# One DMA transpose over 128 partitions and output products in 64x64 tiles for units 3 to 9 of a linear-attention kernel

## The chip, the cores and the metric

The kernel runs on one core of a Trainium2 chip. The core has a matrix engine (TensorE, PE in the profile; its weight loads are listed apart as PEld), VectorE (DVE), ScalarE (ACT), GpSimd (POOL), and SyncE (SP), which here issues most of the DMA transfers. Sixteen DMA engines move the data. The metric is the device time of one execution in microseconds.

## The reference

Two stages follow each other. The first is a gated recurrent attention for 4 sequences of 768 tokens and 8 heads of 48 channels; the state of each head decays by alpha, channel by channel:

```python
for t in range(S):
    state = alpha[:, :, t, :, None] * state + np.einsum('bhd,bhe->bhde', k[:, :, t], v[:, :, t])
    y[:, :, t] = np.einsum('bhd,bhde->bhe', q[:, :, t], state)
```

The second takes y as 3072 rows of 384 channels through a dense pair of layers of 2048 hidden units, with the square of the positive part between them:

```python
h = x @ w_in
r = np.maximum(h, 0.0)
g = r * r
return (g @ w_out).astype(np.float32)
```

Inputs and output are float32; the matrix products inside the kernel run on bfloat16.

## The kernel before

The work is cut into twelve units g of 256 tokens, numbered from 0: unit g is stretch i = g // 4 of sequence g % 4, so units 0 to 3 begin their sequences and units 8 to 11 end them. Within a unit, the partitions hold 128 pairs of neighbouring tokens; j (or jk, for keys) is the place in the pair. A unit has two chunks c of 64 pairs, which lie on partitions 0 to 63 and 64 to 127. Heads go by pairs: p (or n) counts four pairs, x (or rr) the head in the pair.

The steps of a unit, by the names that the prediction uses:

- **Loads** lda, ldk, ldq, ldv (L460): alpha, keys, queries, values, mostly issued by SP.
- **Front**: VectorE multiplies neighbouring alphas (L567), ScalarE takes logarithms (L570), TensorE sums them along the tokens (m1i, L576). From these sums come decay factors, which scale keys and queries into the tile QKS (qks in the profile; L643 and L638). QKS has [side a: keys or queries][j][head][64], 2048 columns on 128 partitions.
- **Transposes** tr0 and tr1 (L654): from unit 3 on, SP issues two DMA transposes, one for each chunk, that is, for 64 partitions by 2048 columns, into KQT (kqt). Each chunk's part of KQT has 1024 columns. KQT has three buffers.
- **Scores** p (L874): products of keys with queries in 64x64 tiles, into psX and psZ, and behind them in the same step the products of keys with values for the state (L727), also in 64x64 tiles with 48 columns. In the last stretch L727 is done for chunk 0 alone. p waits for both transposes.
- **Masks** mk (L891, VectorE): the causal scores into PM (pm).
- **Output** y (L762 and L754): the masked scores with the values ("products", L762), and the queries with the held state ("states", L754). Here a matmul's stationary operand has 64 rows and 128 columns, the 128 tokens of a chunk, and the moving one 48 columns. The row half is that of the chunk for the products and that of the head x for the states. Heads and chunks with x equal to c go to psX, the others to psZ. A unit has 32 products and 16 states; a unit that begins its sequence has 8 states, as chunk 0 has no state before it.
- **Transpose xt** (L932): from unit 4 on, SP transposes the result (128 partitions, 768 columns) for the dense layers; before, TensorE does (L926).
- **Dense layers**: s1 (L989, 128x256 matmuls, six to a step), the positive part (L997) and its square (L1007) on ScalarE, VectorE and GpSimd, s2 (L1035, 128x384 matmuls, four to a step), and the store (L1051).

The order of the work on each engine is written out by hand in TABLES (L206): one list of names for each of the five engines. A planner walks through it, finds for each step the earlier steps that it depends on, and places semaphore waits. SP's list mixes loads, transposes and stores, and SP issues them strictly in that order: a transfer that has to wait holds back all that stand behind it. TensorE's list mixes the attention steps of one unit with the dense steps of earlier ones.

TensorE may run neighbouring matmuls of different row halves side by side. The order in y keeps neighbours on alternating row halves, and a semaphore (swap) holds back the last states until the first products have been added up, since there the row halves change banks.

Of the kernel before, what the change touches and what calls it, by code (L numbers as in the profile page):

```python
# [26 lines left out]
class Program:  # L27
# [145 lines left out]
    def emit(self):  # L173
# [85 lines left out]
        bk5 sd4 vc5 bk6 sd5 sq5_1 vc7 sq8_1 vc10  # L259
    """,  # L260
    "sp": """
        lda0 ldk0 ldq0 ldv0 lda1 ldk1 ldv1 ldq1 lda3 ldk3 ldq3 lda4 ldv3 ldk4 ldq4 ldv4 tr0_3 tr1_3 lda5 tr0_4
        out0_1 tr1_4 ldk5 ldq5 ldv5 lda6 ldk6 tr1_5 tr0_5 out2_1 xt4 ldq6 out1_1 ldv6 lda7 ldq7 ldk7 tr0_6 tr1_6
        xt5 ldv7 out3_1 lda8 ldk8 tr0_7 tr1_7 out4_1 xt6 ldq8 ldv8 lda9 ldq9 ldk9 tr0_8 tr1_8 xt7 ldv9 lda10
        out5_1 ldk10 tr0_9 tr1_9 out6_1 xt8 ldq10 ldv10 lda11 ldk11 tr0_10 tr1_10 out7_1 xt9 ldq11 ldv11 tr0_11
        tr1_11 xt10 out8_1 xt11 out9_1 out10_1 out11_0 out11_10 out11_11
    """,
}
# [18 lines left out]
def bass_gla_recurrent__then__act_relu_squared_kernel(  # L287
# [328 lines left out]
    def front(g):  # L616
        b, i = units[g]
        t0 = i * T
        p0 = FRONT.get(g, (g - 1) * P)
        if g in BY_HEADS:  # L620
            front_by_heads(g, p0)
            return
        r, la, qs, kt, pm, vb, x2 = (g % n for n in (NRAW, 2, NQKS, NKQT, NPM, NV, 2))
        first, last = i == 0, i == NST - 1
        sr, sw = 2 * b + i % 2, 2 * b + (i + 1) % 2

        if g in BY_TOKEN:
# [14 lines left out]
        for a, E, key in ((0, EK, "ek"), (1, EQ, "eq"))[:1 if g in ROW_TILED else 2]:  # L642
            add("dve", lambda e, a=a, E=E: e.tensor_tensor(  # L643
                QKS[qs][:, a, :, :, 0:D], RAW[r][:, 1 + a].rearrange("p h j d -> p j h d"),
                E[la][:].rearrange("p j (h d) -> p j h d", h=H), ALU.mult),
                dve_ns(2 * HD), p0 + 1500 + 100 * a, reads=[("raw", r, 1 + a), (key, la, 0), (key, la, 1)],
                writes=[("qks", qs, a)], name=f"{key}m{g}")

        if g >= PE_TRANSPOSED:

            for c in range(2):
                src = QKS[qs][64 * c:64 * c + 64].rearrange("p a j h d -> p (a j h d)")
                dst = transposed(kt, c).rearrange("p (b s) -> p b s", s=64)
                add("sp", lambda e, dst=dst, src=src: e.dma_start_transpose(dst, src), 1300, p0 + 2500 + c,  # L654
                    reads=[("qks", qs, 0), ("qks", qs, 1)], writes=[("kqt", kt, 0, c), ("kqt", kt, 1, c)], name=f"tr{c}_{g}",
                    dma=f"t{c}_{kt}", lag=1700)
            return

        for a in range(2):
            src = QKS[qs][:, a].rearrange("p j h d -> p (j h d)")  # L660
            bank = psZ[:, a, :].bitcast(BF16)
            psk = [("ps", "Z", a)]

            def tr(pe, src=src, bank=bank):
                for o in range(2 * NPR):
                    ins = pe.matmul(bank[:, o * 128:(o + 1) * 128], src[:, o * 128:(o + 1) * 128], IDENT[:],
                                    is_transpose=True)
                return ins

            add("pe", tr, pe_ns(8, 128), p0 + 2500 + a, reads=[("qks", qs, a), ("ident",)], writes=psk,  # L670
                name=f"tr{a}_{g}")
            dst = KQT[kt][:].rearrange("p a j n s -> p (a j n s)").rearrange("p (c a o s) -> p a o c s", c=2, a=2, s=64)[:, a]
            at = bank.rearrange("p (o c s) -> p o c s", c=2, s=64)
            add("dve", lambda e, dst=dst, at=at: e.tensor_copy(dst, at), dve_ns(1024, 2),
                p0 + 3000 + a, reads=psk, writes=[("kqt", kt, a)], name=f"et{a}_{g}",
                alts={"act": (lambda e, dst=dst, at=at: e.activation(dst, at, AF.Copy), act_ns(1024))})
    def transposed(kt, c):
        return KQT[kt][:].rearrange("p a j n s -> p (a j n s)")[:, c * 1024:c * 1024 + 1024]

    def queries(kt, c, n):  # L680
        return transposed(kt, c)[:, 512 + n * 128:512 + n * 128 + 128]

    def names(g):
        b, i = units[g]
# [55 lines left out]
    def output_row_tiled(g):  # L740


        b, i, sr, sw = names(g)
        kt, pm, vb, x2 = g % NKQT, g % NPM, g % NV, g % 2
        first = i == 0

        def to(p, x, c):
            return psX[:, c, p * D:p * D + D] if x == c else psZ[:, c, p * D:p * D + D]

        def states(pe, tiles, start):  # L750
            for p in range(NPR):
                for x, c in tiles:
                    held = (SMD[x2] if c else SBD[sr])[64 * x:64 * x + 64, p * D:p * D + D]
                    ins = pe.matmul(to(p, x, c), queries(kt, c, p)[64 * x:64 * x + 64], held, start=(start and p == 0),  # L754
                                    stop=False, skip_group_check=True)
            return ins

        def products(pe, tiles, start):
            for p in range(NPR):
                for jk in range(2):  # L760
                    for x, c in tiles:
                        ins = pe.matmul(to(p, x, c), PM[pm][64 * c:64 * c + 64, p // 2, x, p % 2, jk, :],  # L762
                                        VBF[vb][64 * c:64 * c + 64, 2 * p + x, jk, :],
                                        start=(p == 0 and jk == 0 and (start or (first and c == 0))), stop=True,
                                        skip_group_check=True)
            return ins

        def run(pe):
            products(pe, ((1, 0), (0, 1)), True).then_inc(swap, 1)
            swaps[0] += 1  # L770
            states(pe, ((1, 1),) if first else ((0, 0), (1, 1)), True)
            products(pe, ((0, 0), (1, 1)), False)
            pe.wait_ge(swap, swaps[0])
            return states(pe, ((0, 1),) if first else ((0, 1), (1, 0)), False)

        reads = [("pm", pm, 0), ("pm", pm, 1), ("vbf", vb), ("kqt", kt, 1), ("smd", x2)] + ([] if first else [("sbd", sr)])
        return run, 620, reads, [("ps", bank, c) for bank in "XZ" for c in range(2)]
# [75 lines left out]
    def scores(g):  # L853
# [5 lines left out]
        def tiles(hfs):  # L859
            def run(pe):  # L860
                for hf in hfs:
                    psT = halves[hf][0]
                    for nn in range(2):
                        for jk in range(2):
                            for c in range(2):
                                for rr_ in range(2):
                                    n = 2 * hf + nn
                                    o = (nn * 2 + jk) * 128
                                    d0 = 64 * rr_
                                    mov = (queries(kt, c, n)[d0:d0 + 64] if g in ROW_TILED else  # L870
                                           KQT[kt][d0:d0 + 64, 1, :, n, 64 * c:64 * c + 64])
                                    keys = (transposed(kt, c)[d0:d0 + 64, (jk * NPR + n) * 64:(jk * NPR + n) * 64 + 64]
                                            if g in ROW_TILED else KQT[kt][d0:d0 + 64, 0, jk, n, 64 * c:64 * c + 64])
                                    ins = pe.matmul(psT[64 * c:64 * c + 64, rr_, o:o + 128], keys, mov)  # L874
                return ins
            return run
# [238 lines left out]
```

## Time and profile before

| what | value |
|---|---|
| median of 3 runs | 171.86 us (171.46 to 174.43) |
| the profiled execution, whole | 173.53 us |
| its span in the trace | 171.8 us |
| granted TensorE clock, mean | 1.0 |
| DMA transposes issued, L654 and L932 | 18 and 8 |
| matmuls | 2377 |
| output matmuls, L762 and L754 | 352 and 152 |

The profile follows one execution. Its page has the engines' busy time, a strip of 40 equal slices of the span (a digit is the busy share in tenths), the chain of work that ended last, and the costliest groups. Other answers of the trace are used too: a timeline (start, length, engine, line, operation, written tile <- read tiles, shapes, count; in brackets the idle time of the engine just before and what ended it), and the instructions of one line with the time from a DMA's issue to its landing. The end of a matmul in the trace is modelled and overlaps the next one, so its length is no price; the price of a matmul is the distance between starts. L numbers are lines of the kernel before.

### The profile page before, as it was taken

Reading aid. Unit: us, or ns where it says so; the run is one execution under the profiler, and the core shown is the slowest. Engines: PE = TensorE matmul, PEld = TensorE weight load, DVE = VectorE, ACT = ScalarE, POOL = GpSimd, SP = SyncE. Lnnn points to the kernel's source line nnn. Section 1 sums busy time; section 2 is a strip of 40 time slices with the busy share of each in tenths; the row PEclk is TensorE's granted clock in tenths of the full one; section 3 lists DMA queues with packets and bytes.
Section 4 is the critical chain, followed back from the end, with each engine's and each line's share of the span. In section 5 each row is a group of like instructions: output and inputs, shape, how many; then the busy total and the mean of one; then the engine's idle time right before and its main releaser. Section 6 shows DMA issues by size and latency. Waiting matters only on the chain.

```text
span 171.8 us, 5397 instructions
## 1 busy us (share of the span) xinstructions
PE 165.6 (96%) x2377; PEld 128.9 (75%) x2377; DVE 118.2 (69%) x207; ACT 108.9 (63%) x210; POOL 24.2 (14%) x33
## 2 busy tenths in 40 slices
PE   7999999999999999999999999999999999999994
PEld 2556989766877787886768886787788788788773
DVE  5578789888756788975948986887959737432130
ACT  2958689658868278677359567475667464466440
POOL 4052712010252032100240000000420000000000
PEclk9999999999999999999999999999999999999999
DMA  5999999999999999998999998999999582050012
GB/s 143 323 298 186 260 316 219 245 245 288 182 234 209 269 173 211 305 217 146 288 168 211 267 192 153 337 178 243 255 211 205 81 103 85 0 141 0 22 69 92
DMA packets 74743, 33.37 MB, mean 194 GB/s; under 512 B 71648, under 2 KB 71904, under 8 KB 74720
## 3 DMA queue, kind: packets, MB, share of 16 engines
q1 hardware_dynamic: 73184, 28.32, 73.6%
q0 software_dynamic: 1536, 4.72, 12.4%
q8 instruction: 18, 0.29, 0.7%
q14 instruction: 5, 0.04, 0.1%
HBM read 25.17 MB, written 4.72 MB: 174 GB/s over the span
## 4 chain that ended last, share of the span: by engine, by line
PE 58%; DMA 20%; SPq 7%; DVE 6%; ACT 4%; POOL 2%; issue 2%; DVEq 0%
PE psWH L989 25%; PE psO L1035 24%; DMA raw<-in_alpha_dram 7%; DMA wout<-in_moe_w_out_dram 6%; DMA raw<-in_q_dram 4%; SPq L460 3%; DMA raw<-in_k_dram 3%; SPq L654 3%; PE psX L950 2%; POOL raw L460 2%; DVE pm L891 1%; PE psZ L762 1%; PE psX L874 1%; DVE qks L638 1%; DVE qks L643 1%
## 5 line engine op out<-in xcount | busy, mean ns | idle before, releaser
L989 PE MATMUL psWH<-xt,win 128*128 128x256 bf16 x552 | 70.9, 274 | 0.4 <-ACT rr L997 0.3
L989 PEld LDWEIGHTS psWH<-xt,win 128*128 128x128 bf16 x552 | 63.2, 144 | 5.2 <-ACT rr L997 1.1
L1035 PE MATMUL psO<-wout,gt 128*128 128x384 bf16 x352 | 66.7, 326 | 0.0
L997 ACT ACTIVATE rr<-psWH 128x512 bf16<-128x512 f32 x79 | 46.8, 597 | 24.4 <-PE psWH L989 22.9
L1035 PEld LDWEIGHTS psO<-wout,gt 128*128 128x128 bf16 x352 | 32.7, 98 | 16.7 <-DMA wout<-in_moe_w_out_dram 0.2
L1007 DVE TENSOR_TENSOR gt<-rr 128x1024 bf16<-128x1024 bf16 (+1 forms) x46 | 26.6, 584 | 22.0 <-ACT rr L997 21.9
L891 DVE TENSOR_TENSOR pm<-psZ,caus 128x1024 bf16<-128x1024 f32 x12 | 14.6, 1218 | 4.7 <-PE psWH L727 4.1
L1042 ACT ACTIVATE osb<-psO 128x384 f32<-128x384 f32 x17 | 8.3, 491 | 11.7 <-PE psO L1035 11.3
L891 DVE TENSOR_TENSOR pm<-psX,caus 128x1024 bf16<-128x1024 f32 x12 | 14.6, 1218 | 1.0 <-PE psX L874 0.5
L1010 POOL TENSOR_TENSOR gt<-rr 128x1024 bf16<-128x1024 bf16 x3 | 5.7, 1894 | 58.7 <-ACT rr L997 58.7
L643 DVE TENSOR_TENSOR qks<-raw,ek 128x768 bf16<-128x768 f32 x11 | 10.5, 952 | 3.0 <-DMA raw<-in_k_dram 2.5
L638 DVE TENSOR_TENSOR qks<-raw,eq 128x384 bf16<-128x384 f32 x22 | 11.4, 553 | 1.7 <-ACT eq L613 1.0
L1083 PE MATMUL psO<-zero 128*128 128x512 bf16 (+1 forms) x33 | 9.1, 407 | 1.3 <-DVE zero L382 1.3
L999 DVE TENSOR_SCALAR rr<-psWH 128x512 bf16<-128x512 f32 x13 | 8.9, 687 | 1.6 <-PE psWH L989 1.4
L1011 ACT ACTIVATE gt<-rr 128x512 bf16<-128x512 bf16 (+1 forms) x11 | 9.1, 823 | 0.7 <-DVE rr L999 0.4
L910 DVE CAST xbf<-psZ 128x384 bf16<-128x384 f32 x10 | 5.5, 554 | 3.2 <-PE psZ L754 3.2
L634 ACT ACTIVATE vbf<-raw 128x768 bf16<-128x768 f32 x7 | 5.9, 843 | 2.2 <-DMA raw<-in_v_dram 2.1
L567 DVE TENSOR_TENSOR prd<-raw 128x384 f32<-128x384 f32 x9 | 5.7, 636 | 2.1 <-DMA raw<-in_alpha_dram 2.0
L609 ACT ACTIVATE la<-raw 128x384 f32<-128x384 f32 x8 | 4.2, 524 | 4.5 <-DMA raw<-in_alpha_dram 4.5
L570 ACT ACTIVATE lab<-prd 128x384 bf16<-128x384 f32 x10 | 5.2, 521 | 2.4 <-DVE prd L567 2.3
L847 POOL TENSOR_TENSOR sbd<-tmp,acm 128x192 bf16<-128x192 f32 x5 | 2.9, 583 | 25.8 <-DVE tmp L837 22.7
L908 ACT ACTIVATE xbf<-psX 128x384 bf16<-128x384 f32 x11 | 5.3, 482 | 1.9 <-PE psZ L754 1.9
(134 smaller groups left out, 181.5 us busy)
## 6 DMA issues: line engine op xcount, KB each, us to landing
raw<-in_alpha_dram SPq DMA_DIRECT2D x11, 384.0 KB, 5.9
raw<-in_k_dram SPq DMA_DIRECT2D x11, 384.0 KB, 5.8
raw<-in_q_dram SPq DMA_DIRECT2D x11, 384.0 KB, 5.0
raw<-in_v_dram SPq DMA_DIRECT2D x11, 384.0 KB, 5.0
out_dram<-osb SPq DMA_DIRECT2D x11, 384.0 KB, 3.4
win<-in_moe_w_in_dram POOLq DMA_DIRECT2D x2, 768.0 KB, 9.9
wout<-in_moe_w_out_dram POOLq DMA_DIRECT2D x2, 768.0 KB, 11.6
raw<-in_alpha_dram POOLq DMA_DIRECT2D x1, 384.0 KB, 11.1
```

The lines of the kernel that those rows point to most:

```text
L460: load_op[g, nm] = add(ring, lambda e, dst=dst, src=src: e.dma_start(dst, src), cost, (L_PRIO[g] + j if ring == "sp" else W_PRIO[2] + 10 * ...
L638: add("dve", lambda e, j=j, dst=dst: e.tensor_tensor(dst, RAW[r][:, 2, :, j, :].rearrange("p (n x) d -> p n x d", x=2), EQ[la][:, j].rearr ...
L643: add("dve", lambda e, a=a, E=E: e.tensor_tensor(QKS[qs][:, a, :, :, 0:D], RAW[r][:, 1 + a].rearrange("p h j d -> p j h d"), E[la][:].rear ...
L891: add("dve", lambda e, hf=hf, psT=psT: e.tensor_tensor(PM[pm][:, hf].rearrange("p r n j t -> p (r n) (j t)"), psT[:, :, :].rearrange("p r ...
L989: ins = pe.matmul(psN[:, i * T:(i + 1) * T], WIN[:, kk, hidden(fj)], mov, start=(kk == 0), stop=(kk == KT - 1))
L997: add("act", lambda e, psN=psN, rr=rr: e.activation(rr, psN, AF.Relu), act_ns(512), pu + 600, reads=[keyN], writes=[("rr", rb, half)], nam ...
L999: alts={"dve": (lambda e, psN=psN, rr=rr: e.tensor_scalar(rr, psN, 0.0, None, ALU.max), dve_ns(512))})
L1007: add("dve", lambda e, dst=dst, sq=sq: e.tensor_tensor(dst, sq, sq, ALU.mult), 148 + k * 267, pu + 1200, reads=[("rr", rb, h) for h in ran ...
L1011: "act": (lambda e, dst=dst, sq=sq: e.activation(dst, sq, AF.Square), act_ns(k * 512))})
L1035: ins = pe.matmul(psS, GT[gt][:, fj, j, :], WOUT[:, fj, :], start=(fj == 0), stop=(fj == FT - 1))
L1042: add("act", lambda e, j=j, psS=psS: e.activation(OSB[ob][:, j], psS, AF.Copy), act_ns(DM), ps_ + 700, reads=[keyS], writes=[("osb", ob, j ...
L1083: pr.arrange(TABLES, lambda n: lambda pe: pe.matmul(psO[:, 0:n], ZERO[:, 0:128], ZERO[:, 0:n], skip_group_check=True), zero)
```

## The change

For units 3 to 9 (MERGED in the code) the two DMA transposes become one, tr, over all 128 partitions and 2048 columns. KQT then has the plain layout [side][j][head pair][128 pairs of tokens], and both chunks lie side by side in it. Units 10 and 11 keep their two transposes and the layout by chunks. In SP's list tr stands where the first of the two stood; the second is dropped.

In the new layout a chunk's queries for one pair of heads are two runs of 64 columns. As the moving operand of the scores they are read so in one matmul. As the stationary operand of the output's states each run is a matmul of its own, so that states and products of these units now work on 64 columns at a time, in 64x64 tiles: twice as many output matmuls, each still 48 columns wide. The loops are nested so that neighbours still alternate between the row halves, and after each such pair the column half changes.

```diff
@@ TABLES, "sp"
-        lda0 ldk0 ldq0 ldv0 lda1 ldk1 ldv1 ldq1 lda3 ldk3 ldq3 lda4 ldv3 ldk4 ldq4 ldv4 tr0_3 tr1_3 lda5 tr0_4
-        out0_1 tr1_4 ldk5 ldq5 ldv5 lda6 ldk6 tr1_5 tr0_5 out2_1 xt4 ldq6 out1_1 ldv6 lda7 ldq7 ldk7 tr0_6 tr1_6
-        xt5 ldv7 out3_1 lda8 ldk8 tr0_7 tr1_7 out4_1 xt6 ldq8 ldv8 lda9 ldq9 ldk9 tr0_8 tr1_8 xt7 ldv9 lda10
-        out5_1 ldk10 tr0_9 tr1_9 out6_1 xt8 ldq10 ldv10 lda11 ldk11 tr0_10 tr1_10 out7_1 xt9 ldq11 ldv11 tr0_11
+        lda0 ldk0 ldq0 ldv0 lda1 ldk1 ldv1 ldq1 lda3 ldk3 ldq3 lda4 ldv3 ldk4 ldq4 ldv4 tr_3 lda5 tr_4
+        out0_1 ldk5 ldq5 ldv5 lda6 ldk6 tr_5 out2_1 xt4 ldq6 out1_1 ldv6 lda7 ldq7 ldk7 tr_6 
+        xt5 ldv7 out3_1 lda8 ldk8 tr_7 out4_1 xt6 ldq8 ldv8 lda9 ldq9 ldk9 tr_8 xt7 ldv9 lda10
+        out5_1 ldk10 tr_9 out6_1 xt8 ldq10 ldv10 lda11 ldk11 tr0_10 tr1_10 out7_1 xt9 ldq11 ldv11 tr0_11
@@ front
-            for c in range(2):
-                src = QKS[qs][64 * c:64 * c + 64].rearrange("p a j h d -> p (a j h d)")
-                dst = transposed(kt, c).rearrange("p (b s) -> p b s", s=64)
...
+            if g not in MERGED:
+                for c in range(2):
...
+                return
+            src = QKS[qs][:].rearrange("p a j h d -> p (a j h d)")
+            dst = KQT[kt][:].rearrange("p a j n s -> p (a j n) s")
+            add("sp", lambda e, dst=dst, src=src: e.dma_start_transpose(dst, src), 1300, p0 + 2500,
+                reads=[("qks", qs, 0), ("qks", qs, 1)], writes=[("kqt", kt, 0), ("kqt", kt, 1)], name=f"tr_{g}",
+                dma=f"t_{kt}", lag=1700)
             return
...
+    MERGED = range(PE_TRANSPOSED, 10)
+
+    def key_columns(g, c, n, jk):
+        kt = g % NKQT
+        if g in ROW_TILED and g not in MERGED:
+            o = 1024 * c + (jk * NPR + n) * 64
+            return KQT[kt][:].rearrange("p a j n s -> p (a j n s)")[:, o:o + 64]
+        return KQT[kt][:, 0, jk, n, 64 * c:64 * c + 64]
+
+    def queries(g, c, n):
...
+        return KQT[kt][:, 1].rearrange("p j n s -> p (j n s)").rearrange("p (n j c s) -> p n j c s", n=NPR, j=2, c=2)[:, n, :, c, :]
@@ output_row_tiled
-        def to(p, x, c):
-            return psX[:, c, p * D:p * D + D] if x == c else psZ[:, c, p * D:p * D + D]
+        wide = g not in MERGED
+        parts = ((0, 128),) if wide else ((0, 64), (64, 128))
+
+        def to(p, x, c, lo, hi):
+            return (psX if x == c else psZ)[lo:hi, c, p * D:p * D + D]

         def states(pe, tiles, start):
             for p in range(NPR):
-                for x, c in tiles:
-                    held = (SMD[x2] if c else SBD[sr])[64 * x:64 * x + 64, p * D:p * D + D]
-                    ins = pe.matmul(to(p, x, c), queries(kt, c, p)[64 * x:64 * x + 64], held, start=(start and p == 0),
-                                    stop=False, skip_group_check=True)
+                for part, (lo, hi) in enumerate(parts):
+                    for x, c in tiles:
+                        held = (SMD[x2] if c else SBD[sr])[64 * x:64 * x + 64, p * D:p * D + D]
+                        q = queries(g, c, p)[64 * x:64 * x + 64]
+                        ins = pe.matmul(to(p, x, c, lo, hi), q if wide else q[:, part], held, start=(start and p == 0),
+                                        stop=False, skip_group_check=True)
             return ins

         def products(pe, tiles, start):
             for p in range(NPR):
                 for jk in range(2):
-                    for x, c in tiles:
-                        ins = pe.matmul(to(p, x, c), PM[pm][64 * c:64 * c + 64, p // 2, x, p % 2, jk, :],
...
+                    for lo, hi in parts:
+                        for x, c in tiles:
+                            ins = pe.matmul(to(p, x, c, lo, hi), PM[pm][64 * c:64 * c + 64, p // 2, x, p % 2, jk, lo:hi],
...
```

More of the change, by code (lines that the diff above doesn't have):

```diff
@@ L649, in front @@
         if g >= PE_TRANSPOSED:
-            for c in range(2):
-                src = QKS[qs][64 * c:64 * c + 64].rearrange("p a j h d -> p (a j h d)")
-                dst = transposed(kt, c).rearrange("p (b s) -> p b s", s=64)
-                add("sp", lambda e, dst=dst, src=src: e.dma_start_transpose(dst, src), 1300, p0 + 2500 + c,
-                    reads=[("qks", qs, 0), ("qks", qs, 1)], writes=[("kqt", kt, 0, c), ("kqt", kt, 1, c)], name=f"tr{c}_{g}",
-                    dma=f"t{c}_{kt}", lag=1700)
+            if g not in MERGED:
+                for c in range(2):
+                    src = QKS[qs][64 * c:64 * c + 64].rearrange("p a j h d -> p (a j h d)")
+                    dst = KQT[kt][:].rearrange("p a j n s -> p (a j n s)")[:, c * 1024:c * 1024 + 1024].rearrange("p (b s) -> p b s", s=64)
+                    add("sp", lambda e, dst=dst, src=src: e.dma_start_transpose(dst, src), 1300, p0 + 2500 + c,
+                        reads=[("qks", qs, 0), ("qks", qs, 1)], writes=[("kqt", kt, 0, c), ("kqt", kt, 1, c)], name=f"tr{c}_{g}",
+                        dma=f"t{c}_{kt}", lag=1700)
+                return
[4 more added lines that the diff above has]
+                dma=f"t_{kt}", lag=1700)
             return
@@ L676, in front @@
                 alts={"act": (lambda e, dst=dst, at=at: e.activation(dst, at, AF.Copy), act_ns(1024))})
[L677 to L681, printed above, removed]
+    MERGED = range(PE_TRANSPOSED, 10)
[6 more added lines that the diff above has]
+    def queries(g, c, n):
+        kt = g % NKQT
+        if g not in ROW_TILED:
+            return KQT[kt][:, 1, :, n, 64 * c:64 * c + 64]
+        if g not in MERGED:
+            o = 1024 * c + 512 + n * 128
+            return KQT[kt][:].rearrange("p a j n s -> p (a j n s)")[:, o:o + 128]
+        return KQT[kt][:, 1].rearrange("p j n s -> p (j n s)").rearrange("p (n j c s) -> p n j c s", n=NPR, j=2, c=2)[:, n, :, c, :]
     def names(g):
@@ L760, in products @@
                 for jk in range(2):
-                    for x, c in tiles:
[L762 to L765, printed above, removed]
+                    for lo, hi in parts:
+                        for x, c in tiles:
+                            ins = pe.matmul(to(p, x, c, lo, hi), PM[pm][64 * c:64 * c + 64, p // 2, x, p % 2, jk, lo:hi],
+                                            VBF[vb][64 * c:64 * c + 64, 2 * p + x, jk, :],
+                                            start=(p == 0 and jk == 0 and (start or (first and c == 0))), stop=True,
+                                            skip_group_check=True)
             return ins
@@ L869, in run @@
                                     d0 = 64 * rr_
[L870 to L873, printed above, removed]
+                                    mov = queries(g, c, n)[d0:d0 + 64]
+                                    keys = key_columns(g, c, n, jk)[d0:d0 + 64]
                                     ins = pe.matmul(psT[64 * c:64 * c + 64, rr_, o:o + 128], keys, mov)
```

## The prediction

> **What bounds the kernel now.** I read the page first: busy times, the strip of 40 slices, the chain that ended last.
>
> ```profile
> span 171.8 us, 5397 instructions
> ...
> PE 165.6 (96%) x2377; PEld 128.9 (75%) x2377; DVE 118.2 (69%) x207; ACT 108.9 (63%) x210; POOL 24.2 (14%) x33
> ...
> DMA  5999999999999999998999998999999582050012
> ...
> PE 58%; DMA 20%; SPq 7%; DVE 6%; ACT 4%; POOL 2%; issue 2%; DVEq 0%
> ```
>
> TensorE is busy 96% of the span, and the chain is mostly TensorE; but the DMA engines are full until about slice 31 (133 us), and DMA with SP's queue holds 27% of the chain. So two resources run nearly level. A busy share cannot say which one pays, so next I asked the chain, in order of time, for the price of a dense matmul:
>
> ```profile
> 104.35 2.60 PE psO L1035 x16
> ...
> 128.08 1.31 PE psWH L989 x12
> ```
>
> A 384-wide L1035 costs 2.60 / 16 = 0.1625 us, a 256-wide L989 1.31 / 12 = 0.109 us. With these the timeline of TensorE shows how long it really stands still, from one group's start to the next group's:
>
> ```profile
> 40.51 0.81 PE L1035 MATMUL psO<-wout,gt 128*128 128x384 bf16 x4
> 41.49 0.34 PE L576 MATMUL psWH<-lab,linc 128*128 128x384 bf16 x1 [0.17 <-ACT lab L570]
> ...
> 47.16 0.82 PE L989 MATMUL psWH<-xt,win 128*128 128x256 bf16 x6
> 48.11 0.42 PE L874 MATMUL psX<-kqt 64*64 64x128 bf16 x16
> ...
> 59.67 1.47 PE L989 MATMUL psWH<-xt,win 128*128 128x256 bf16 x12
> 61.52 0.37 PE L762 MATMUL psZ<-vbf,pm 64*128 64x48 bf16 x16 [0.38 <-DVE pm L891]
> ...
> 78.97 1.46 PE L1035 MATMUL psO<-wout,gt 128*128 128x384 bf16 x8
> 80.83 0.42 PE L874 MATMUL psX<-kqt 64*64 64x128 bf16 x16 [0.40 <-ACT eq L613]
> ...
> 87.67 0.88 PE L989 MATMUL psWH<-xt,win 128*128 128x256 bf16 x6
> 88.80 0.34 PE L576 MATMUL psWH<-lab,linc 128*128 128x384 bf16 x1 [0.24 <-ACT lab L570]
> ```
>
> Work that switches the array from 128x128 to a smaller tile adds 0.09 us (worked out below). Taking the work and, where there is one, the switch from each distance leaves the stalls: before m1i4 0.98 - 0.65 = 0.33; before p3 0.95 - 0.65 - 0.09 = 0.21; before y4 1.85 - 1.31 - 0.09 = 0.45; before p6 1.86 - 1.30 - 0.09 = 0.47; before m1i8 1.13 - 0.66 = 0.47. From 40 us on the timeline has no other gap of that size. So TensorE sets the pace, and it has about 1.9 us of stalls to give, nothing after 89 us. Whatever the change adds to TensorE after that point is paid in full.
>
> **The tiles, which cost.** These rows are y7 (output), p7 (scores, then L727, which already uses 64x64 tiles), p8's L727 and y3:
>
> ```profile
> 98.03 0.37 PE L762 MATMUL psZ<-vbf,pm 64*128 64x48 bf16 x16
> 98.25 0.18 PE L754 MATMUL psX<-sbd,kqt 64*128 64x48 bf16 x1
> ...
> 98.35 0.36 PE L762 MATMUL psX<-vbf,pm 64*128 64x48 bf16 x16
> 98.55 0.18 PE L754 MATMUL psZ<-smd,kqt 64*128 64x48 bf16 x1
> ...
> 98.74 0.66 PE L989 MATMUL psWH<-xt,win 128*128 128x256 bf16 x4
> ...
> 93.19 0.42 PE L874 MATMUL psX<-kqt 64*64 64x128 bf16 x16
> ...
> 93.66 0.42 PE L727 MATMUL psWH<-vbf,qks 64*64 64x48 bf16 x32
> 94.01 0.82 PE L1035 MATMUL psO<-wout,gt 128*128 128x384 bf16 x4
> ...
> 108.08 0.41 PE L727 MATMUL psWH<-vbf,qks 64*64 64x48 bf16 x16
> 108.42 0.99 PE L1035 MATMUL psO<-wout,gt 128*128 128x384 bf16 x5
> ...
> 51.65 0.37 PE L762 MATMUL psZ<-vbf,pm 64*128 64x48 bf16 x16
> ...
> 52.28 0.34 PE L576 MATMUL psWH<-lab,linc 128*128 128x384 bf16 x1
> ```
>
> y7 takes 98.74 - 98.03 = 0.71 us for 48 matmuls. Its first eight L754 take 0.10 (98.25 to 98.35), its last eight, with the change of tile behind them, 0.19: the switch is 0.09, the rest 0.62 us, 12.9 ns a matmul. The change cuts each into two halves of 64 output rows: 96 matmuls of 64x64 tiles, 48 columns wide. That exact shape, with neighbours on alternating row halves and then on the other column half, is L727 in p7: 0.35 us for 32, less 0.09, is 8.1 ns. So y becomes 96 x 8.1 ns + 0.09 = 0.87 us: +0.16 us a unit. Bounds: nothing, if the halves ran fully side by side; and 15.6 ns a matmul, the price of p8's L727, all of whose matmuls sit on one row half ((0.34 - 0.09) / 16): 96 x 15.6 + 0.09 = 1.59 us, +0.88 us a unit. I take 8.1 ns, the row with the same order. Units 4 to 9 give 6 x 0.16 = 0.96 us. Unit 3 is the first of its sequence and has no state products for the first chunk: 40 matmuls in 0.63 us (51.65 to 52.28), so 0.54 without the switch. Of its 80 the 64 products cost 64 x 8.1 = 0.52, and the 16 state products have one row half alone: between 16 x 8.1 and 16 x 15.6, 0.13 to 0.25. That is +0.11 to +0.23, taken as 0.17. Sum on TensorE: **+1.13 us**.
>
> [...]
>
> The scores of p now read their queries as two runs of 64 columns instead of one of 128. Unit 0 reads them so already:
>
> ```profile
> 11.18 0.42 PE L874 MATMUL psZ<-kqt 64*64 64x128 bf16 x16
> 11.53 0.34 PE L542 MATMUL psWH<-laf,linc 128*128 128x384 bf16 x1
> ```
>
> (0.35 - 0.09) / 16 = 16 ns, start of the burst included; p7's 32, from 93.19 to 93.66, take 14.7. I take no cost, as a start is spread over 16 there and over 32 here (bounds 0 and 32 x 1.3 ns = 0.04 us a unit).
>
> **The transposes, which gain.** Seven pairs of DMA transposes (64 partitions, 2048 columns each) become seven single ones over 128 partitions. The same bytes move, but SP issues one less each, and nothing is moved past another wait: both halves waited for the same two writes of qks. Rows of SP's queue and of landing, kqt first, then xt, which is already a 128-partition transpose (768 columns):
>
> ```profile
> L654 SPq DMA_TRANSPOSE kqt<-qks x18: 1247/1734/4367, 41.4 to 135.3; - x18
> DMA to landing us min/median/max: 3.7/4.5/6.5
> L932 SPq DMA_TRANSPOSE xt<-xbf x8: 1211/1264/2142, 64.3 to 149.7; - x8
> DMA to landing us min/median/max: 2.7/3.2/3.7
> 73.39 4.53 SPq L654 DMA_TRANSPOSE kqt<-qks  x2
> ```
>
> The second of a pair starts at the soonest one shortest issue, 1.25 us, behind the first, and lands 3.7 to 4.5 us after its own start: 5.0 to 5.8 us for a pair that nothing holds up. The merged one has no row. Lower bound: xt, 2.7 us for 768 columns. Upper: two medians in a row, 9.0. Scaling what xt needs beyond its issue, 2.7 - 1.2 = 1.5 us, by 2048 / 768 gives 4.0, plus 1.2 of issue: 5.2 us. Scaled xt is the nearest row, as its tiles have the same 128 rows; but the fixed part of its 1.5 us is scaled too, so I expect some 0.5 us less, 4.7. The pair of unit 6 (73.39, 4.53 us of issue in a full queue) ends at 77.92; its second, begun about 1.3 earlier and landing 3.7 to 4.5 later, is there at 80.3 to 81.1, and p6 starts at 80.83. So p6 waits for the landing, and p3 likewise: its second transpose starts at 44.03 (next rows), is there at 47.7 to 48.5, and p3 starts at 48.11. Half a microsecond is enough to end both stalls: -0.21 - 0.47 = -0.68 us.
>
> Behind the pairs queue the loads:
>
> ```profile
> 44.03 1.35 SPq L654 DMA_TRANSPOSE kqt<-qks  x1
> ...
> 49.91 1.35 SPq L654 DMA_TRANSPOSE kqt<-qks  x1
> ...
> 56.93 0.96 DVE L643 TENSOR_TENSOR qks<-raw,ek 128x768 bf16<-128x768 f32 x1 [2.48 <-DMA raw<-in_k_dram]
> ...
> 87.62 0.56 DVE L567 TENSOR_TENSOR prd<-raw 128x384 f32<-128x384 f32 x1 [1.22 <-DMA raw<-in_alpha_dram]
> ```
>
> The second transpose of unit 4 (49.91) goes, so the keys of unit 5 are issued up to 1.35 us sooner; VectorE sat idle 2.48 us for them at 56.93, and what it does from there to 61.5 is the scores' mask that y4 waits for. In the same way alpha of unit 8, for which VectorE waited 1.22 us at 87.62, feeds m1i8. Up to 0.45 + 0.47 = 0.92 us more; the DMA engines are full, so a sooner issue need not be a sooner landing, and I take 0.7. The gain is 0.68 + 0.7 = 1.4 us. What is late next is TensorE itself.
>
> The profiled execution took 173.53 us, 1.7 around its span of 171.8; the median of the runs, 171.86, lies 1.67 below it. The sum, +1.13 - 1.4 = -0.27, makes that execution 173.3 and the median **171.6 us**. 2% is 3.4 us, about what a measurement of this kernel can tell from no change.
>
> **The rivals.**
> 1. *The loads and landings don't come sooner.* For it: a full DMA strip. Against: fewer issues, and the 1.35 us of SP. Then the stalls swallow part of the tiles' cost: what units 3 to 6 add lies before m1i8, and only y7 to y9 pay in full, 3 x 0.16 = 0.48 us, 172.3; if the stalls move along with TensorE, the whole 1.13, 173.0.
> 2. *All stalls go.* Besides the five, the waits of TensorE's weight loads from 40 us on (total us, times, longest) show small ones on ScalarE:
>
> ```profile
> PEld psWH L989 <- ACT rr L997: 0.7, 3, 0.3
> ```
>
> Then 1.9 + 0.7 - 1.13 = 1.5 us off, 170.4. Against: m1i4 waits for a VectorE chain older than the first merged transpose.
> 3. *The 64x64 tiles don't overlap* (the other side). PM and the transposed queries would load as p8's L727 does, 15.6 ns a matmul: 6 x 0.88 + (80 x 15.6 ns - 0.54 = 0.71) = 6.0 us, less the 1.4: 176.5. It decides above 2% from (0.62 + (3.4 + 1.4) / 7) / 96 = 13.6 ns a matmul. For: no run of small tiles in the trace is longer than p's 64 matmuls, and y would have 96. Against: L727's 8.1 ns at the end of those 64. [...]
> 4. *The merged transpose lands later than the pair*, at the 9.0 us bound: 9.0 - 5.4 = 3.6 us late for p3 and p6 each, which wait for it now: 2 x 3.6 + 1.13 = 8.3 us, 180.2. Against: xt's 2.7.
>
> **How the numbers follow.** Forecast 0.55; rival 1 0.27; rival 2 0.08; rival 3 0.05; rival 4 0.03; 0.02 for a gain that no stall here shows, the only way to be faster by over 2% (1.9 + 0.7 us of stalls are less than 3.4). The likeliest case itself spans 171.2 to 172.1. The range takes rivals 1 and 2 in: 170.4, and 173.0 plus 0.4 for the scatter that the three runs show (171.46 and 171.86 at their nearest): 173.4. Left out are rivals 3 and 4 and the rest, 0.1. Faster 0.02, within 2% 0.90, slower 0.08.
>
> **What would show it.** y7 at 0.87 us from its first L762 to the next group; one transpose a unit with an issue of 1.2 to 3.4 us; p3 and p6 without a stall before them; VectorE's waits for the keys of unit 5 and alpha of unit 8 shorter by about a microsecond; after 89 us the same spacing of dense groups, y7 to y9 longer. A y of 1.1 us or more, or a new stall before the scores, proves it wrong.

## The result, and the profile after

The changed kernel takes 173.79 us (median of 22 runs, 172.68 to 174.51); the kernel before, run beside it, 173.24 us (22 runs). The ratio is 1.0059 with a 95% interval of 1.0033 to 1.0085, that is, 1.0 us more (0.6 to 1.5): no difference by the 2% rule, but on the slow side, where the sum had forecast 0.27 us less, and above the range of 170.4 to 173.4 us. The ratio leaves out five of the 22 runs of the kernel before, those over 1.5% above its fastest; the medians of all runs differ by 0.55 us. The page of the changed kernel, whose profiled execution took 173.36 us:

```profile
span 171.6 us, 6042 instructions
...
PE 166.6 (97%) x2705; PEld 130.7 (76%) x2705; DVE 119.0 (69%) x207; ACT 108.5 (63%) x210; POOL 24.6 (14%) x33
...
DMA  5999999999999978999998999959697552040012
...
q8 instruction: 21, 0.34, 0.8%
...
PE 80%; DMA 10%; DVE 3%; SPq 2%; ACT 2%; issue 1%; POOL 0%
```

DMA and SP's queue held 27% of the chain before and hold 12% now; TensorE went from 58% to 80%. The path is shorter where transfers set it and longer where TensorE does. The timeline of TensorE shows both (products are L787 and states L778 in the new numbering, scores L897, s1 L1012, s2 L1058):

```profile
46.83 0.82 PE L1012 MATMUL psWH<-xt,win 128*128 128x256 bf16 x6
47.58 0.42 PE L897 MATMUL psX<-kqt 64*64 64x128 bf16 x16
...
51.12 0.44 PE L787 MATMUL psZ<-vbf,pm 64*64 64x48 bf16 x32
...
51.96 0.34 PE L576 MATMUL psWH<-lab,linc 128*128 128x384 bf16 x1
...
59.58 1.47 PE L1012 MATMUL psWH<-xt,win 128*128 128x256 bf16 x12
60.98 0.44 PE L787 MATMUL psZ<-vbf,pm 64*64 64x48 bf16 x32
...
61.79 0.19 PE L778 MATMUL psZ<-sbd,kqt 64*64 64x48 bf16 x1
61.91 0.55 PE L1012 MATMUL psWH<-xt,win 128*128 128x256 bf16 x3
...
78.92 1.46 PE L1058 MATMUL psO<-wout,gt 128*128 128x384 bf16 x8
80.31 0.42 PE L897 MATMUL psX<-kqt 64*64 64x128 bf16 x16
...
87.37 0.88 PE L1012 MATMUL psWH<-xt,win 128*128 128x256 bf16 x6
88.09 0.33 PE L576 MATMUL psWH<-lab,linc 128*128 128x384 bf16 x1
```

Taken as in the prediction, the stalls before p3 (47.58 - 46.83 - 0.65 - 0.09), y4 (60.98 - 59.58 - 1.31 - 0.09), p6 (80.31 - 78.92 - 1.30 - 0.09) and m1i8 (88.09 - 87.37 - 0.66) are 0.01, 0.00, 0.00 and 0.06 us: gone. (The 0.06 is no stall: of the six dense matmuls behind the small tiles of y6 the first takes 0.06 us longer than the others. The 0.47 us before m1i8 in the kernel before has the same 0.06 in it.) But y4 takes 61.91 - 60.98 = 0.93 us and y3 0.84, where y7 took 0.71 and y3 0.63 before: +0.21 us, not +0.16.

The single transposes hold SP for 1.5 to 3.3 us each, as was said of them; to land they take 5.2 us in the middle, where 4.7 was expected. Their own line, and VectorE's row for the step that waited 2.48 us for the keys of unit 5:

```profile
L661 SPq DMA_TRANSPOSE kqt<-qks x7: 1497/3090/3343, 40.8 to 107.6; - x7
...
DMA to landing us min/median/max: 4.3/5.2/6.7
```

```profile
56.23 1.03 DVE L638 TENSOR_TENSOR qks<-raw,eq 128x384 bf16<-128x384 f32 x2 [1.22 <-DMA raw<-in_q_dram]
```

VectorE no longer waits there for keys; its wait is for queries, and half as long. For alpha of unit 8 (1.22 us before) it does not wait any more.

### The profile page after: what moved, and what is told of

Its sections match the earlier page's. It is cut to its first block, busy times and chain, and to the rows that moved or that the text cites. A ratio compares the mean times of both kernels' runs of the same rounds, so it can differ in the third digit from the quotient of the medians.

```text
span 171.6 us, 6042 instructions
## 1 busy us (share of the span) xinstructions
PE 166.6 (97%) x2705; PEld 130.7 (76%) x2705; DVE 119.0 (69%) x207; ACT 108.5 (63%) x210; POOL 24.6 (14%) x33
## 3 DMA queue, kind: packets, MB, share of 16 engines
q1 hardware_dynamic: 72960, 28.32, 71.3%
## 4 chain that ended last, share of the span: by engine, by line
PE 80%; DMA 10%; DVE 3%; SPq 2%; ACT 2%; issue 1%; POOL 0%
PE psO L1058 34%; PE psWH L1012 31%; DMA wout<-in_moe_w_out_dram 7%; DMA raw<-in_alpha_dram 3%; PE psX L897 2%; PE psZ L787 2%; SPq L460 2%; PE psZ L897 2%; PE psX L787 2%; PE psX L973 2%; PE psWH L1058 2%; DVE pm L914 1%; PE psWH L746 1%; PE psWH L576 1%; PE psZ L778 1%
## 5 line engine op out<-in xcount | busy, mean ns | idle before, releaser
L1012 PE MATMUL psWH<-xt,win 128*128 128x256 bf16 x552 | 70.7, 274 | 0.2
L1058 PE MATMUL psO<-wout,gt 128*128 128x384 bf16 x352 | 66.9, 327 | 0.4 <-DMA wout<-in_moe_w_out_dram 0.4
L1012 PEld LDWEIGHTS psWH<-xt,win 128*128 128x128 bf16 x552 | 63.4, 144 | 4.6 <-ACT rr L1020 0.4
L1058 PEld LDWEIGHTS psO<-wout,gt 128*128 128x128 bf16 x352 | 32.7, 98 | 17.3 <-DMA wout<-in_moe_w_out_dram 0.7
L567 DVE TENSOR_TENSOR prd<-raw 128x384 f32<-128x384 f32 x9 | 6.6, 733 | 1.4 <-DMA raw<-in_alpha_dram 1.4
L1106 PEld LDWEIGHTS psO<-zero 128*128 128x128 bf16 x33 | 3.0, 107 | 4.3 <-issue 1.7
```

Source lines behind the costliest of these rows:

```text
L1012: ins = pe.matmul(psN[:, i * T:(i + 1) * T], WIN[:, kk, hidden(fj)], mov, start=(kk == 0), stop=(kk == KT - 1))
L1058: ins = pe.matmul(psS, GT[gt][:, fj, j, :], WOUT[:, fj, :], start=(fj == 0), stop=(fj == FT - 1))
L1106: pr.arrange(TABLES, lambda n: lambda pe: pe.matmul(psO[:, 0:n], ZERO[:, 0:128], ZERO[:, 0:n], skip_group_check=True), zero)
```

## The experiments

Two theories first. **A**: the 64x64 tiles cost about 0.21 us a unit, always; the single transposes only take stalls away, and a usual execution of before has fewer of them than the profiled one. **B**: the tiles' cost vanishes in stalls, and the single transposes themselves cost. A later one, **C**, asks whether the gain is spread over all seven units.

**e1: the changed kernel again**, unchanged.

> The changed kernel itself, for a second look at where its executions lose time. Theory A (the tiles cost a fixed 1.5 us, 7 x 0.21 us a unit by the changed kernel's trace; the single transposes only take away stalls of TensorE, and the typical execution of the kernel before has fewer of them than the profiled one): ratio to before 1.004 to 1.008, y about 0.92 us in every unit, few stalls before p3, y4, p6 and m1i8. Theory B (the tiles are nearly swallowed, and the single transpose costs: it makes loads land later): the same ratio, but new stalls on DMA landings before 90 us, of 0.5 us and more in sum.

174.6 us, ratio 1.0102 (1.0042 to 1.0162): slower, as before. Its profiled execution took 176.18 us, and its trace is used for places alone.

**e2: the transposes alone.** The products and states stay whole. In the single transpose's layout no 128-wide run of a chunk's queries exists, so that the states of the seven units read other columns of the same tile; the output is not the reference's.

```diff
-        wide = g not in MERGED
+        wide = True
...
-                        q = queries(g, c, p)[64 * x:64 * x + 64]
+                        q = (KQT[kt][:, 1, c, p, :] if g in MERGED else queries(g, c, p))[64 * x:64 * x + 64]
```

> Units 3 to 9 with one transpose, but the output matmuls in 64x128 tiles as before; the held state is multiplied with other columns of the transposed queries than it should be, so the output isn't the reference's; instructions, sizes and order are those of before. Theory A: faster than before by what the stalls are worth, 0.5 to 1.3 us (ratio 0.992 to 0.997), y back at 0.71 us. Theory B: same or slower than before (1.000 to 1.006).

171.6 us, ratio 0.9944 (0.9912 to 0.9976), that is, -0.97 us (-1.5 to -0.4). Twelve runs lie between 171.39 and 172.53, while those of before reach 171.35 at their fastest and 172.85 in the middle: the single transposes bring every run near the best that before has.

**e3: the tiles alone.** The kernel before, with its pairs of transposes, and the halved loops of the change in units 3 to 9.

```diff
+        wide = g not in range(3, 10)
+        parts = ((0, 128),) if wide else ((0, 64), (64, 128))
...
-                for x, c in tiles:
+                for lo, hi in parts:
+                    for x, c in tiles:
...
```

> Units 3 to 9 with output matmuls in 64x64 tiles, but the two transposes and the layout of before. Theory A: slower than before by 0.64 us (units 7 to 9, behind the last stall, 3 x 0.21) up to 1.5 us (all seven units): ratio 1.004 to 1.009, and stalls as in before. Theory B: 0.2 to 0.7 us, ratio 1.001 to 1.004.

174.37 us, ratio 1.0092 (1.0056 to 1.0128): +1.6 us (1.0 to 2.2). With e2's -1.0 that makes +0.6, at the lower end of the interval of the change as a whole. B falls: the tiles cost and the transposes gain. The trace of e2 gives the tiles' price free of stalls. In the changed kernel the products of y3 begin at 51.12 (above) and those of y10, which has whole tiles, at 136.60; the second fence has both for e2:

```profile
136.60 0.37 PE L787 MATMUL psZ<-vbf,pm 64*128 64x48 bf16 x16
```

```profile
51.27 0.30 PE L787 MATMUL psZ<-vbf,pm 64*128 64x48 bf16 x10
...
134.90 0.37 PE L787 MATMUL psZ<-vbf,pm 64*128 64x48 bf16 x16
```

85.48 us against 83.63: seven units with halved tiles cost 1.85 us here, of which 7 x 0.21 = 1.47 is the longer y. The rest is looked for below.

**e4: halve the states only.** The change halves the states, since the layout has a chunk's queries in two runs; the products need not follow. Products of 128 columns would leave 64 matmuls in a y instead of 96.

```diff
-                    for lo, hi in parts:
+                    for lo, hi in ((0, 128),):
```

> The change, but the products of the masked scores with the values stay in 64x128 tiles; only the state products are halved, as the layout asks for. Theory A: y has 32 x 12.5 + 32 x 8 ns and a change of tile inside, at most 3 x 0.09 us more: 0.75 to 1.0 us; at 0.75 the time is 1.2 us less than the change's (ratio to before 0.998), at 1.0 it is 0.5 us more (1.009). Theory B: as the change, 1.004 to 1.008, whatever y takes.

174.32 us, ratio 1.0101 (1.0066 to 1.0135): no cheaper than the change. Part of y7 in its timeline (16 whole products, 16 halved states, then the same again; the dense work follows at the last row):

```profile
97.20 0.37 PE L787 MATMUL psZ<-vbf,pm 64*128 64x48 bf16 x16
97.50 0.21 PE L778 MATMUL psX<-sbd,kqt 64*64 64x48 bf16 x1
...
97.63 0.19 PE L778 MATMUL psX<-smd,kqt 64*64 64x48 bf16 x1
97.75 0.37 PE L787 MATMUL psX<-vbf,pm 64*128 64x48 bf16 x16
...
98.30 0.88 PE L1012 MATMUL psWH<-xt,win 128*128 128x256 bf16 x6
```

y7 takes 1.10 us. From the last halved state to the first whole product pass 0.12 us, where neighbours of one shape stand 0.01 apart: this change from 64x64 to 64x128 tiles costs about 0.11 us. This order has three changes between them in a y; at the other two, from whole products to halved states, the first product and the first state start 0.30 us apart, where y7 of before has 0.22 and 0.20, so that they cost 0.08 and 0.10. One shape throughout, with more matmuls, is the cheaper way here: 1.01 us in y7 of the changed kernel.

**e5: only the units whose stalls the prediction named**, 3, 4 and 6, in the new form; the others keep the old one, and SP's list has their pairs of transposes again.

```diff
-    MERGED = range(PE_TRANSPOSED, 10)
+    MERGED = (3, 4, 6)
```

> The change in units 3, 4 and 6 alone, whose transposes and loads stood ahead of the stalls in the profiled execution of before. Theory A (each unit with 64x64 tiles costs 0.21 us wherever it stands, and the single transposes gain where TensorE waits, before 90 us): 0.64 us for the tiles, less 0.7 to 1.0 of stalls: ratio to before 0.997 to 1.000, below the whole change's 1.006. Rival C (the gain is spread over all seven transposes, as each frees the DMA engines): three sevenths of the gain, 0.4 us, and ratio 1.001 to 1.003.

172.75 us, ratio 1.0014 (0.9969 to 1.0059): not told apart from before, nor, at its upper end, from the change.

**e6: the tiles in all units that can take them**, 1 to 11, with the old transposes.

```diff
+        wide = False
+        parts = ((0, 128),) if wide else ((0, 64), (64, 128))
```

> Output matmuls in 64x64 tiles in units 1 to 11 instead of 3 to 9, two transposes as before. Theory A: four units more at 0.21 us, 0.8 us over the seven units alone (1.009): ratio to before 1.012 to 1.016. If the 1.6 us of the seven units alone were mostly something that comes once (another program, other timing of the first loads): 1.008 to 1.011.

176.75 us, ratio 1.0228 (1.0170 to 1.0285): +3.9 us. Theory A's 11 x 0.21 = 2.3 us is too little. The rest stands in y1:

```profile
21.49 0.19 PE L759 MATMUL psZ<-smd,kqt 64*64 64x48 bf16 x1
21.50 0.19 PE L768 MATMUL psX<-vbf,pm 64*64 64x48 bf16 x1
23.46 0.27 PE L759 MATMUL psZ<-smd,kqt 64*64 64x48 bf16 x6 [1.77 <-issue]
```

In the middle of a y 1.96 us pass from one matmul's start to the next one's, 1.77 of them idle, and the release is "issue": nothing that the profile shows was waited for. States into psZ from the same tiles had run just before.

**e7 and e8: before and the changed kernel once more**, beside e5 and e6, for a second trace of each.

> The kernel before, unchanged, for a second look at its stalls. Both theories: ratio 1.000 within 0.004. Theory A: the stalls before p3, y4, p6 and m1i8 are there again but of another sum, between 0 and 3 us, as the times of the runs scatter over that much.

> The changed kernel, unchanged, for another look. Ratio 1.003 to 1.009. Theory A: stalls between 45 and 90 us of 0.5 us at most in sum; what its executions scatter comes from the time before 20 us, ahead of all that was changed.

Before 173.11 us, ratio 1.0000 (0.9959 to 1.0042); the changed kernel 173.94 us, 1.0067 (1.0030 to 1.0104). In the second trace of before, y4, p6 and m1i8 look so:

```profile
59.53 1.47 PE L989 MATMUL psWH<-xt,win 128*128 128x256 bf16 x12
60.97 0.37 PE L762 MATMUL psZ<-vbf,pm 64*128 64x48 bf16 x16
...
79.80 1.46 PE L1035 MATMUL psO<-wout,gt 128*128 128x384 bf16 x8
81.19 0.42 PE L874 MATMUL psX<-kqt 64*64 64x128 bf16 x16
...
88.03 0.88 PE L989 MATMUL psWH<-xt,win 128*128 128x256 bf16 x6
89.03 0.34 PE L576 MATMUL psWH<-lab,linc 128*128 128x384 bf16 x1
```

The stalls before y4 and p6, 0.45 and 0.47 us in the first trace, are 0.04 and 0.00 here, and p3's, 0.21, is 0.01 (dense work from 47.22, p3 at 47.97); only that before m1i8 stays, 1.00 - 0.66 = 0.34.

In the changed kernel the stall before p3 comes back. The trace of e8 has 0.13 us there, and those of e9 and e12 (below), which leave the computation as it is, 0.15 and 0.26. It is a wait for the single transpose of unit 3, here in e12:

```profile
47.01 0.82 PE L1012 MATMUL psWH<-xt,win 128*128 128x256 bf16 x6
...
48.01 0.42 PE L897 MATMUL psX<-kqt 64*64 64x128 bf16 x16 [0.18 <-DMA kqt<-qks]
```

From its issue to its landing that transpose takes 6.2 us in the first trace of the changed kernel, 6.5 in e8 and 6.6 in e9 and e12. The pair, from the first issue to the second landing, took 6.6, 6.4 and 6.2 us in the traces of before, e7 and e10: for unit 3 the single transpose lands no sooner.

Other gaps of before stand elsewhere in its second trace, and one of them is again an "issue" inside a y, here y5:

```profile
72.88 0.18 PE L754 MATMUL psZ<-sbd,kqt 64*128 64x48 bf16 x1
73.52 0.18 PE L754 MATMUL psZ<-smd,kqt 64*128 64x48 bf16 x1 [0.46 <-issue]
```

**What the unexplained gaps have in common.** The page lists a queue of its own for instructions, with packets of 16 KB (0.34 MB in 21):

```profile
q8 instruction: 18, 0.29, 0.7%
```

That is before: 2 x 2377 = 4754 (the counts of the page) matmuls and weight loads by 18 packets, 264 each; the changed kernel has 5410 by 21, 258 each. By that count TensorE's program comes in pieces of some 256 instructions, and the gaps below lie multiples of 256 apart, to within five. Counted in the traces, in instructions of TensorE from its first (matmuls, weight loads and the waits for semaphores), the gaps stand at these places:

| kernel | place | from start to start, us | instruction | over a multiple of 256 | the 256 before, us |
|---|---|---|---|---|---|
| e6 | y1 | 1.96 | 701 | 189 | 3.7 |
| e6 | y3 | 0.49 | 1725 | 189 | 3.8 |
| e5 | p4 | 0.49 | 1724 | 188 | 5.1 |
| changed kernel | p4 | 0.24 | 1728 | 192 | 5.1 |
| e8 | p4 | 0.19 | 1724 | 188 | 5.1 |
| e7 | y5 | 0.64 | 2236 | 188 | 5.2 |
| e3 | y5 | 0.27 | 2492 | 188 | 4.9 |

e1's trace, taken for the places alone, has two, in p4 at 1724 and, 0.9 us long, in y5 at 2493. The steps differ and the kernels differ; the place modulo 256 does not, to within the few records that a trace can miss. The last column, the time in which the 256 instructions up to there were used, is short in all of them (the whole program averages 171.8 / 18 = 9.5 us a piece before); at some 5 us other edges pass without a gap, so y5 of before in its first trace, and in e9 and e12 (below) edges at 4.1 and 4.6 us do. Hence theory **F**: small matmuls use up a piece of the program faster than the next one comes. Its rival **G**: the gaps belong to the step, by a landing or a wait there. Three kernels move the program against the edges and leave the computation as it is, by replacing some fills (matmuls on zeros ahead of the first s1) of 512 columns with more, short ones of 2 columns.

```diff
-        +512 +512 +512 +512 +512 +512 +512 +512 m10_0
+        +512 +512 +512 +512 +512 +512 +512 +2 +2 +2 +2 +2 +2 +2 +2 +2 +2 +2 +2 m10_0
```

This is e11's; e9, e10 and e12 do the same with other counts.

**e9: the changed kernel moved by 152 instructions.**

> The changed kernel with its computation untouched; of the fills ahead of the first s1, some of 512 columns are replaced by 76 more pairs of two columns, so that every later instruction of TensorE stands 152 places further down the program. Theory F (TensorE's program is fetched in pieces of 256 instructions, and a run of small matmuls that uses up a piece faster than the next arrives stands still at the piece's edge): the gaps of 0.2 to 0.9 us that the changed kernel's traces show after p4 and in y5 are gone, and a new one of 0.5 to 2 us stands in y3, where an edge now falls 256 instructions and some 3.8 us behind the one before it; smaller ones of 0 to 0.9 us in y7 or y8. Ratio to before 1.007 to 1.015. Theory G (the gaps belong to the step, by a landing or a wait there, and not to a place in the program): the gaps stay after p4 and in y5, none appears in y3, and the ratio stays at 1.004 to 1.008.

**e12: the same, for a second trace.**

> The kernel of the run before last that was moved by 152, once more, for a second trace. Theory F: the gap stands in y3 again, at the same matmul, 0.3 to 2 us long, and none after p4 or in y5; the distance from y3 to y10, 85.5 us in the traces of the changed kernel without the move, is longer by the gap less the 0.2 us that went after p4. Theory G: the gap in y3 was an accident of one execution; y3 takes 0.85 us and y3 to y10 85.3 to 85.6 us.

e9: 174.46 us (one of its twelve runs took 333.84 us, and why is not known), ratio 1.0082 (1.0048 to 1.0115), inside F's range, but not outside the interval of the unmoved kernel; the ratio alone decides nothing. The one run of e12 took 175.35 us. The places decide. y3 in e9, then y3, p4 and y10 in e12:

```profile
52.02 0.43 PE L787 MATMUL psX<-vbf,pm 64*64 64x48 bf16 x26
53.96 0.21 PE L787 MATMUL psX<-vbf,pm 64*64 64x48 bf16 x2 [1.51 <-issue]
```

```profile
51.54 0.44 PE L787 MATMUL psZ<-vbf,pm 64*64 64x48 bf16 x32
...
51.92 0.43 PE L787 MATMUL psX<-vbf,pm 64*64 64x48 bf16 x26
53.87 0.21 PE L787 MATMUL psX<-vbf,pm 64*64 64x48 bf16 x2 [1.52 <-issue]
...
58.34 0.39 PE L897 MATMUL psZ<-kqt 64*64 64x128 bf16 x16
58.57 0.42 PE L746 MATMUL psWH<-vbf,qks 64*64 64x48 bf16 x32
...
138.59 0.37 PE L787 MATMUL psZ<-vbf,pm 64*128 64x48 bf16 x16
```

In both, the gap has gone to y3, between the same two matmuls, 1.7 us long (53.96 - 52.02, less 26 matmuls of 8.5 ns), at instruction 1729, with 3.8 us for the 256 before: where the gap of the unmoved kernel stood, though another step is there now. After p4 there is none: 0.23 us from the scores in psZ to the state products, where the changed kernel has 0.42:

```profile
56.16 0.63 PE L897 MATMUL psZ<-kqt 64*64 64x128 bf16 x16
56.58 0.45 PE L746 MATMUL psWH<-vbf,qks 64*64 64x48 bf16 x32
```

From y3 to y10 e12 takes 138.59 - 51.54 = 87.05 us, 1.57 more than the changed kernel: 1.7 gained, 0.2 lost. What the DMA engines did in e12 from 51.3 to 52.5 us:

```profile
q1 hardware_dynamic: 213, 0.38, 103.3%
q8 instruction: 1, 0.02, 6.0%
```

One packet of instructions, 6.0% of 16 engines for 1.2 us, so 1.15 us long on its engine, in a stretch in which the engines are full; 1.4 us after its end TensorE goes on. In all the other gaps named here, e1's and e10's with them, TensorE likewise goes on 1.3 to 1.6 us after the end of such a packet, however long the gap. G falls: the gaps go with the place in the program and end with the arrival of a piece. F's other half, that the speed of the small matmuls opens them, fits the four edges reached within 3.8 us, two in e6 and one each in e9 and e12, which all have a gap. At 4.1 to 5.5 us some have one and some have none, and what delays a packet there is not shown.

**e10 and e11: before moved by 36, and e5's kernel moved by 22**, meant to keep the edges out of the small matmuls.

> The kernel before with 18 more pairs of fills of two columns in place of two fills of 512 ahead of the first s1, so that every later instruction of TensorE stands 36 places further down. Theory F: no edge of a piece falls into a stretch of small matmuls, so that the gap of 0.64 us in y5, which one of two traces of before showed, cannot occur; the stalls ahead of p3, y4, p6 and m1 stay. Ratio 0.996 to 1.000. Theory G: 1.000, with a gap in y5 in some executions.

> The single transpose and the 64x64 products in units 3, 4 and 6 alone, with 11 more pairs of fills of two columns in place of one fill of 512 ahead of the first s1, so that every later instruction of TensorE stands 22 places further down. Theory F: the gap of 0.49 us after p4 that the unmoved version showed is gone and no other takes its place: ratio to before 0.995 to 1.000, against 1.0014 unmoved. Theory G: the gap stays after p4, ratio 1.000 to 1.003.

Counted as in the table, the moves did not do that: an edge still falls into y5 in e10, with 5.7 us for the 256 before, and into p4 in e11, with 5.0 us. TensorE passes both without a gap, so that these two runs do not decide about F.

e10: 174.02 us, ratio 1.0025 (0.9977 to 1.0074). Its trace has a gap in another step, the transpose of y1 on TensorE, at instruction 705, 193 over a multiple of 256:

```profile
22.81 0.33 PE L926 MATMUL psX<-ident,xbf 128*128 128x128 bf16 x3
23.32 0.34 PE L926 MATMUL psX<-ident,xbf 128*128 128x128 bf16 x3 [0.17 <-issue]
```

The runs are not faster than before, and how often a run of before has a gap is not known. It also shows the prediction's stalls a third time. In its timeline the last dense group starts at 46.76 before p3 at 47.51, at 59.07 before y4 at 60.48, at 77.91 before p6 at 79.30 and at 86.15 before m1i8 at 87.14; less the work and the switch that leaves 0.01, 0.01, 0.00 and 0.33 us.

e11: 173.04 us, ratio 0.9977 (0.9938 to 1.0016), against 1.0014 for e5; the gap in p4 is gone from its trace, though an edge is still there. The intervals overlap, so the gain of the move is not shown, and neither is one over the kernel before. C, too, stays open. No correct version was found that is measurably faster than before; e2 gives the bound for one whose states read the layout whole.

## Why the prediction was wrong

Right: the mechanism, in both directions. The transposes gain, by a shorter SP queue and by stalls that vanish before y4, p6 and m1i8 in every trace of the changed kernel, though not before p3; the tiles cost, on TensorE, in full. The failed step is the balance "+1.13 - 1.4 = -0.27", and both of its terms were off, to the same side.

1. **"So y becomes 96 x 8.1 ns + 0.09 = 0.87 us": too small.** It takes 0.93 in y4 (y7, which the prediction named, has 1.01, from 97.21 to 98.22, with one more gap of 0.07 before its last two matmuls, the cause of which is not known): (61.79 - 60.98) / 95 = 8.5 ns from matmul to matmul, and 0.12 from the last one to the dense work, 0.11 of it the change of tile. Of the 0.06 us more, 0.02 is the change of tile, taken as 0.09, and the rest the spacing: 8.1 ns was right for the first 32 products, but the last 32 stand 8.6 apart, the states 6.9 and 8.3, and between these four groups lie 0.01 to 0.02 us. Why the spacings differ is not known. Seven times 0.21 is 1.5 us instead of 1.13.
2. **"no run of small tiles in the trace is longer than p's 64 matmuls, and y would have 96"** stood in rival 3 as the reason for it, and the rival was set aside since the tiles overlap. They do: 8.5 ns, or 34 for four matmuls with their weight loads, is far from the 13.6 at which it would decide. But the longer run has another limit, the supply of instructions. It adds 0.2 us in the profiled execution and up to 1.96 in e6, and with the 1.5 us it fits the +1.6 us of e3. The prediction has no term for it. What shows it are the packets of 16 KB, one to 258 or 264 matmuls and weight loads, and the gaps 188 to 193 instructions over a multiple of 256; that a run of short instructions outruns the supply rests on the four edges reached within 3.8 us.
3. **"The gain is 0.68 + 0.7 = 1.4 us": too large**; e2 measures 0.97 (0.4 to 1.5). In the profiled execution the stalls were there, and the change ends them. But those before p3, y4 and p6 are not a trait of the kernel: two further traces, of before (e7) and of before with moved fills (e10), have 0.04 us or less at all three. Only the stall before m1i8 is in each, 0.33 to 0.47 us. The prediction took one execution's stalls for every execution's. Its step for p3, "Half a microsecond is enough to end both stalls", also failed on the landing: the single transpose of unit 3 lands 6.2 to 6.6 us after its issue, as the pair did, and p3 waits for it in three of four traces.
4. **The base.** 171.86 us was the median of three runs, 171.46, 171.86 and 174.43; that of 22 is 173.24. Of the 2.2 us between forecast and result 1.4 are this. The prediction saw that its profiled execution stood 1.67 us above the median and subtracted that; with 173.24 the distance is 0.29.

Of the other rivals, the first (no relief) is refuted by e2, the second (all stalls go) came true for the stalls of the profiled execution but not for the time, and the fourth by p6, which starts without a wait, and p3, which waits 0.26 us at most in these traces where the rival asks for 3.6.

Still open: how the gaps of the instruction supply are spread over the executions of each kernel, since each trace shows one; and which of the seven transposes earn the gain.

## What to carry to other kernels

A stall seen in one profiled execution is a sample: before it is put down as a gain, look for it in a second trace, and weigh it against the scatter of the runs. Price a changed run of small matmuls with its own spacing, the change of tile behind it and its length, and keep one tile shape throughout, for each change inside it cost 0.08 to 0.11 us here, as much as 9 to 13 of the matmuls. Where a change doubles the number of short instructions, count them per piece of 256: 256 used up in under 4 us cost 0.5 to 2 us here, and in 4 to 5.5 us from nothing to 0.6 (0.9 in e1); moving the edge by many cheap instructions shows whether they do.

## What the runs showed of the hardware

- **The supply of instructions.** Gaps of 0.19 to 1.96 us from start to start, with no wait behind them, stand in ten traces, all 188 to 193 instructions over a multiple of 256 in TensorE's program. Moving the program by 152 moves them (e9, e12), and each ends 1.3 to 1.6 us after a packet of instructions.
- **A change of tile shape** costs 0.08 to 0.11 us also between 64x64 and 64x128, in the middle of small matmuls (e4).
- **Four 64x64 tiles with their weight loads** take 34 ns over runs of 96, joins included (y4 of the changed kernel). Of L727 in p7 of before, on both row halves, four start 3 to 4 ns apart and the next four follow 18 to 22 ns later; in p8, on one row half, two start 6 to 7 ns apart and the next two follow 22 to 25 ns later.
- **The wider transpose takes less of the DMA engines' time.** The pages give the same 28.32 MB on the hardware queue in every kernel, but 73.6% of sixteen engines over 171.8 us before, or 126.4 us on each, and 71.3% over 171.6 us, or 122.3, in the changed kernel. The five traces with pairs in all units lie at 126.2 to 130.2 us, the six with single transposes in seven units at 118.0 to 125.3 (without e1's).
